# First stage of the transforms in the quarters of TensorE's array, two groups of four matmuls in one visit

## The chip, the cores and the metric

The kernel runs on one core of one Trainium2 chip. The metric is the device time of one execution in microseconds (us), as the median of several runs. TensorE multiplies matrices, ScalarE (ACT) and VectorE (DVE) work on elements, GpSimd (POOL) and SyncE (SP) here mostly issue transfers.

## The reference

For each of 8 batches, x (3008 x 256) is transformed along the sequence, multiplied by a filter and transformed back; then a layer with a leaky activation follows.

```python
X = np.fft.rfft(x, axis=1)
Y = X * (filt_r + 1j * filt_i)[None]
y = np.fft.irfft(Y, n=3008, axis=1)       # 8 x 3008 x 256
h = y.reshape(24064, 256) @ w_in          # 24064 x 2048
g = np.maximum(h, 0) + alpha * np.minimum(h, 0)
out = g @ w_out                           # 24064 x 256
```

## The kernel before, in words

**The transforms.** The length 3008 is split into 47 x 64. A transform (class `Fft`, one for each batch after the first, which `First` does in its own way) has four stages. *Stage a* multiplies by a DFT matrix of length 47 (cosines and sines of 24 frequencies: 48 columns). An x tile `xs` holds a chunk: 8 of the 32 positions of one half of the 64, for both halves h, in 2 x 47 = 94 rows. `piece_a` (L237) is one matmul of 94 rows by 96 columns (a block-diagonal matrix `wf1_s`, one block for each h) over 512 columns of x, into a bank of the pool psF (L245). ScalarE evicts it (`on_act`, L324) into the tile `asb`. Four pieces make a chunk, four chunks a transform, so 7 x 16 = 112 pieces; `save_a` (L249) stores a chunk to `a_dram` from SP, and `turn_a` loads it back turned. *Stage b* (`piece_b`, L265) and the filter (`scale`, L278, with two accumulating transfers on POOL, L281), *stage c* (`piece_c`, L292) and *stage d* (`piece_d`, four matmuls at L317, evicted into `yT`) follow, each in psF banks, two of which alternate (`bank`, L218).

**The layer.** It runs in 47 blocks of 512 rows. `up(j)` (L613), 16 times a block, makes two matmuls of 512 columns (L618; four shorter ones where a block wraps in `yT`) into one half of a tile of the pool `psH` (name hps, two buffers of two banks); after the second of a pair ScalarE evicts both halves at once (L634, 1024 columns), VectorE makes the bent part (`m_s`, L640; ScalarE L638 for one j), and adds it (L821). The second product, `items()`, has two forms. A block whose digit in `KINDS` is a dot takes `eight()`: 64 matmuls of 256 columns (L669). A block with a digit takes `seven()`: seven half-size products in place of eight, 112 matmuls of 128 columns (L691), with sums on VectorE (L650, L652, L658, L594) and some on POOL (L656), and five evictions of 256 columns (L703 to L718). `SUMS` says, for each digit, at which step which sum is made. 38 of the 47 blocks have a digit.

**The order.** It is written out by hand. A step is one `up`. At each step the program emits what is late, the sums, then what `plan` holds for this step (pieces of transforms, stores, loads), then `up(j)`, then as many products of an earlier block as keep the products `LAG` (17) steps behind. `PLACES` holds for each transform the steps of the pieces of a, b, c and d relative to its start (94 steps a batch); `LOADS` those of the loads of x (POOL); `STEPS_*` those of the first transform and of the setup. Each engine works in order, so a piece that waits holds up all that comes after it on its engine.

Of the kernel before, what the change touches and what calls it, by code (L numbers as in the profile page):

```python
# [10 lines left out]
FP16 = mybir.dt.float16  # L11
# [3 lines left out]
N1 = 47  # L15
# [35 lines left out]
)  # L51
STEPS_T = (0, 0, 1, 2, 5, 8, 11, 26, 28, 30, 32, 33)
STEPS_E = (4, 7, 10, 12, 27, 29, 31, 31, 40, 45, 49, 51)
STEPS_N = (34, 37, 38, 23)
STEPS_F = (29, 14, 15, 4, 15)
STEPS_K = (37, 40, 47, 58, 40)
LOADS = (
# [6 lines left out]
)  # L64
KINDS = "...1201.3310001.100000100000001001.00.0000000.."
SUMS = (
# [46 lines left out]
def kernel(  # L113
# [12 lines left out]
    wf1_d = nc.inline_tensor(wf1_np.astype(np.float16), name="c_wf1")  # L126
# [35 lines left out]
    wf1_s = konst.tile([2 * N1, 96], FP16, name="wf1_s")  # L162
# [34 lines left out]
    def load_x(b, c, halves=(0, 1)):  # L197
        if 0 in halves:
            xc[(b, c)] = p_x.tile([2 * N1, 8 * D], FP16, name="xs")
        for h in halves:  # L200
            nc.gpsimd.dma_start(out=xc[(b, c)][h * N1 : h * N1 + N1], in_=xrow(b, h, c))  # L201
# [29 lines left out]
    class Fft:  # L231
# [5 lines left out]
        def piece_a(self, i, evict, wide=False):  # L237
            if i == 0:
                self.at = p_fft.tile([128, NK1, D], FP16, name="at")
            if i % 4 == 0:  # L240
                self.asb[i // 4] = p_as.tile([96, 8, D], FP16, name="asb")
            xs = xc[(self.b, i // 4)]
            ps = bank(wide)
            o = (i % 4) * 512
            nc.tensor.matmul(ps[0:96], wf1_s, xs[:, o : o + 512], start=True, stop=True)  # L245
            u = 2 * (i % 4)
            evict(self.asb[i // 4][:, u : u + 2].rearrange("p a d -> p (a d)"), ps[0:96])

        def save_a(self, c):  # L249
            nc.sync.dma_start(out=a_dram[self.b, :, 8 * c : 8 * c + 8], in_=self.asb[c])  # L250
# [516 lines left out]
    for b in range(1, NB):  # L767
# [3 lines left out]
        for i in range(16):  # L771
            put(p + steps_a[i], f.piece_a, i, on_act)
            if i % 4 == 3:
                put(p + steps_a[i] + (b > 2), f.save_a, i // 4)
# [110 lines left out]
```

## Time and profile before

| | |
|---|---|
| median of 3 runs | 761.08 us (760.99 to 761.57) |
| the profiled execution | 761.13 us, of which 759.3 us span |
| granted TensorE clock | 1.00 |
| matmuls | 7812 |
| stage a: matmuls L245; evictions L324 into asb | 112, 381 ns each; 112, 593 ns each (median) |
| L618 and its evictions L634 | 1600 matmuls; 376 of 1028 ns |
| L691 (seven products), L669 (eight) | 4256 and 512 matmuls |
| VectorE, ScalarE, POOL busy | 694.4, 673.5, 162.9 us |

A row of a group of instructions gives line, engine, operation, output and inputs, shape and count, then busy time, mean duration of one, and the idle time of the engine just before. A matmul's duration holds the latency of the pipeline: from start to start a 512-column matmul takes 0.22 us, though its row says 0.38. The first 34 us are the first transform and the loading of weights; from there the blocks run.

### The profile page before, as it was taken

The page shows a single profiled execution, that of the slowest core. Times are in us where ns is not written, and L with a number is a line of the kernel's source. Part 1 is how long each engine was busy: PE and PEld are TensorE (multiplying, and loading weights), DVE is VectorE, ACT ScalarE, POOL GpSimd, SP SyncE. Part 2 cuts the span into 40 slices and gives each one's busy share as a digit, 9 for nine tenths or more (in the row PEclk, how much of TensorE's full clock was granted, in tenths as well). Part 3 has the DMA queues.
Part 4 walks back from the last instruction along what each step waited for, and adds up shares of the span by engine and source line. Part 5 has one row for each costly group of instructions (what it writes and reads, how often), then busy time and mean ns, then how long its engine had stood idle before and what let it go on. Part 6 is the DMA issues. An engine that isn't in the chain of part 4 may idle for free.

```text
span 759.3 us, 19855 instructions
## 1 busy us (share of the span) xinstructions
PE 743.7 (98%) x7812; PEld 539.3 (71%) x7812; DVE 694.4 (91%) x1298; ACT 673.5 (89%) x1083; POOL 162.9 (21%) x236
## 2 busy tenths in 40 slices
PE   7989999999999999999999999999999999999998
PEld 5746666776787777776778777777777777777766
DVE  5787887998999998899999999999998998999994
ACT  6888999999999998999899998999989898888873
POOL 8631421232022221232022211221100221010100
PEclk9999999999999999999999999999999999999999
DMA  8995888778975596766876659865586355522122
GB/s 158 196 236 157 148 179 217 173 147 167 206 156 118 117 186 172 153 119 142 186 161 144 138 117 204 186 134 115 106 181 137 78 104 113 139 64 65 44 64 62
DMA packets 100790, 107.97 MB, mean 142 GB/s; under 512 B 10568, under 2 KB 81496, under 8 KB 100696
## 3 DMA queue, kind: packets, MB, share of 16 engines
q1 hardware_dynamic: 80136, 70.05, 36.1%
q0 software_dynamic: 20416, 36.58, 29.7%
q8 instruction: 61, 1.00, 0.6%
q14 instruction: 33, 0.27, 0.1%
q10 hardware_dynamic: 144, 0.07, 0.0%
HBM read 55.41 MB, written 46.66 MB: 134 GB/s over the span
## 4 chain that ended last, share of the span: by engine, by line
PE 91%; ACT 1%; DVE 1%; issue 0%; DVEq 0%; ACTq 0%
PE hps L618 42%; PE op L691 31%; PE op L669 7%; PE psF L245 3%; PE psF L317 3%; PE psF L265 2%; PE psF L292 2%; PE op L723 1%; ACT gtb L634 1%; ACT v L324 0%; PE hps L723 0%; DVE m_s L640 0%; ACT asb L324 0%; ACT yT L324 0%; PE psF L426 0%
## 5 line engine op out<-in xcount | busy, mean ns | idle before, releaser
L618 PE MATMUL hps<-yT,win_s 128*128 128x512 f16 (+3 forms) x1600 | 447.6, 366 | 0.4 <-ACT yT L324 0.4
L634 ACT ACTIVATE gtb<-hps 128x1024 f16<-128x1024 f32 x376 | 386.1, 1028 | 50.6 <-PE hps L618 47.8
L691 PEld LDWEIGHTS <-gtb 128*128 128x128 f16 x3040 | 206.0, 98 | 100.0 <-issue 1.0
L640 DVE TENSOR_SCALAR m_s<-gtb,alm_s 128x512 f16<-128x512 f16 x705 | 215.0, 351 | 37.4 <-ACT gtb L634 34.0
L821 DVE TENSOR_TENSOR gtb<-gtb,m_s 128x2048 f16<-128x2048 f16 x188 | 229.8, 1223 | 5.3 <-ACT m_s L638 3.2
L691 PE MATMUL op<-wout_s,gtb 128*128 128x128 f16 x1824 | 153.2, 219 | 0.0
L618 PEld LDWEIGHTS <-win_s 128*128 128x128 f16 x1600 | 135.2, 98 | 24.7 <-issue 3.3
L281 POOL DMA_DIRECT2D uw_s<-uw_s x84 | 72.4, 1002 | 330.4 <-DVE uw_s L278 206.3
L691 PEld LDWEIGHTS <-ss 128*128 128x128 f16 x1216 | 83.1, 98 | 37.4
L691 PE MATMUL op<-tw_s,gtb 128*128 128x128 f16 x1216 | 105.0, 219 | 0.0
L691 PE MATMUL op<-tw_s,ss 128*128 128x128 f16 x1216 | 103.4, 219 | 0.0
L669 PE MATMUL op<-wout_s,gtb 128*128 128x256 f16 x512 | 76.9, 272 | 0.3 <-DVE osb L594 0.3
L656 POOL DMA_DIRECT2D gtb<-gtb x28 | 27.7, 990 | 207.9 <-ACT gtb L634 139.6
L669 PEld LDWEIGHTS <-gtb 128*128 128x128 f16 x512 | 50.0, 98 | 31.3
L324 ACT ACTIVATE asb<-psF 96x512 f16<-96x512 f32 x112 | 65.7, 601 | 1.8 <-PE psF L245 0.9
L324 ACT ACTIVATE yT<-psF 128x376 f16<-128x376 f32 x118 | 56.8, 494 | 5.5 <-PE psF L317 4.6
L324 ACT ACTIVATE v<-psF 128x512 f16<-128x512 f32 x88 | 52.0, 603 | 3.8 <-PE psF L292 2.7
L278 DVE TENSOR_TENSOR uw_s<-uw_s,filt 128x2048 f16<-128x2048 f16 x42 | 51.3, 1221 | 2.9 <-DMA uw_s<-uw_s 2.4
L201 POOL DMA_DIRECT2D xs<-in_x_dram x64 | 51.8, 974 | 5.0 <-issue 2.4
L269 ACT ACTIVATE uw_s<-psF 128x512 f16<-128x512 f32 x84 | 50.0, 605 | 2.9 <-PE psF L265 2.0
L652 DVE TENSOR_TENSOR ss<-ss,gtb 128x1024 f16<-128x1024 f16 x76 | 52.1, 686 | 0.1
L650 DVE TENSOR_TENSOR ss<-gtb 128x1024 f16<-128x1024 f16 (+1 forms) x75 | 52.0, 693 | 0.0
(125 smaller groups left out, 643.7 us busy)
## 6 DMA issues: line engine op xcount, KB each, us to landing
out_dram<-osb SPq DMA_DIRECT2D x127, 128.0 KB
xs<-in_x_dram POOLq DMA_DIRECT2D x64, 188.0 KB, 5.4
a_dram<-asb SPq DMA_DIRECT2D x28, 384.0 KB
uw_s<-uw_s POOLq DMA_DIRECT2D x84, 128.0 KB, 3.6
v_dram<-v SPq DMA_DIRECT2D x112, 96.0 KB
zt<-v_dram SPq DMA_DIRECT2D x28, 384.0 KB
at<-a_dram SPq DMA_DIRECT2D x20, 384.0 KB
gtb<-gtb POOLq DMA_DIRECT2D x28, 256.0 KB, 3.8
```

The costliest lines, as they stand in the source:

```text
L201: nc.gpsimd.dma_start(out=xc[(b, c)][h * N1 : h * N1 + N1], in_=xrow(b, h, c))
L278: nc.vector.tensor_mul(w.rearrange("p (i d) -> p i d", d=1024)[:, 0 : iu // 2 + 1 : iu // 2], uu.unsqueeze(1).to_broadcast([128, 2, 1024]), f)
L281: nc.gpsimd.dma_start(out=uu[o : o + 64], in_=ww[64 - o : 128 - o], accum_op=OP.add)
L324: nc.scalar.activation(o, i, AF.Copy)
L618: nc.tensor.matmul(self.hps[:, j % 2, ca:cb], win_s[:, kt, j * 128 : (j + 1) * 128], yT[:, kt, at : at + cb - ca], start=(kt == 0), stop=( ...
L634: nc.scalar.activation(g, hs, AF.Copy)
L640: nc.vector.tensor_scalar(ms[:, i], g[:, i], 0.0, a, OP.min, OP.mult)
L650: nc.vector.tensor_add(z1, a21, a22)
L652: nc.vector.tensor_add(z2, z1, a11)
L669: nc.tensor.matmul(op[:, si % 2], self.pair(k // 2)[:, k % 2, 128 * si : 128 * si + 128], wout_s[:, k], start=(k == 0), stop=(k == 15))
L691: nc.tensor.matmul(acc[:, 128 * i : 128 * i + 128], x[:, k, 128 * i : 128 * i + 128], b[:, k], start=first and k + i == 0, stop=k == 7, sk ...
L821: nc.vector.tensor_add(g, g, ms)
```

## The change

Stage a is done chunk by chunk. `xs` and the matrix lie in rows 0 to 46 and 64 to 110, one half h in each, and the matrix has 64 columns (48 and 16 of zeros). `piece_a(c)` now makes eight matmuls of 47 rows by 64 columns over 512 columns of x: two groups (j) of four, where each of the four has its own half of the rows (h) and of the columns (u), so that a group covers the four quarters of the array. The first group writes both banks of a tile of psH, the second both banks of psF. ScalarE evicts the first at once (1024 columns), the second in two. All of it is emitted in one visit at the step where the chunk's last piece stood. `asb` has 128 rows; `save_a` stores it with two transfers in place of one. There are 28 visits.

```diff
-    wf1_d = nc.inline_tensor(wf1_np.astype(np.float16), name="c_wf1")
+    wfq_np = np.zeros((2, 64, 64))
+    wfq_np[:, 0:N1, 0:48] = wf1_np[0:N1, 0:48]
+    wf1_d = nc.inline_tensor(wfq_np.reshape(128, 64).astype(np.float16), name="c_wf1")
...
-            nc.gpsimd.dma_start(out=xc[(b, c)][h * N1 : h * N1 + N1], in_=xrow(b, h, c))
+            o = h * (64 if b else N1)
+            nc.gpsimd.dma_start(out=xc[(b, c)][o : o + N1], in_=xrow(b, h, c))
...
-        def piece_a(self, i, evict, wide=False):
-            if i == 0:
+        def piece_a(self, c):
+            if c == 0:
                 self.at = p_fft.tile([128, NK1, D], FP16, name="at")
-            if i % 4 == 0:
-                self.asb[i // 4] = p_as.tile([96, 8, D], FP16, name="asb")
-            xs = xc[(self.b, i // 4)]
-            ps = bank(wide)
-            o = (i % 4) * 512
-            nc.tensor.matmul(ps[0:96], wf1_s, xs[:, o : o + 512], start=True, stop=True)
-            u = 2 * (i % 4)
-            evict(self.asb[i // 4][:, u : u + 2].rearrange("p a d -> p (a d)"), ps[0:96])
+            self.asb[c] = p_as.tile([128, 2, 4, D], FP16, name="asb")
+            hp = psH.tile([128, 2, 512], FP32, name="hps")
+            for j, ps in enumerate(((hp[:, 0], hp[:, 1]), (bank(), bank()))):
+                for u in range(2):
+                    for h in range(2):
+                        r = slice(64 * h, 64 * h + N1)
+                        o = 1024 * u + 512 * j
+                        nc.tensor.matmul(ps[h][64 * u : 64 * u + 64], wf1_s[r], xc[(self.b, c)][r, o : o + 512],
+                                         start=True, stop=True)
+                a = self.asb[c][:, :, 2 * j : 2 * j + 2].rearrange("p h a d -> p h (a d)")
+                if j == 0:
+                    nc.scalar.activation(a, hp, AF.Copy)
+                else:
+                    for h in range(2):
+                        nc.scalar.activation(a[:, h], ps[h], AF.Copy)
 
         def save_a(self, c):
-            nc.sync.dma_start(out=a_dram[self.b, :, 8 * c : 8 * c + 8], in_=self.asb[c])
+            for u in range(2):
+                s = 8 * c + 4 * u
+                nc.sync.dma_start(out=a_dram[self.b, :, s : s + 4].rearrange("(h m) s d -> m h s d", h=2),
+                                  in_=self.asb[c][64 * u : 64 * u + 48])
...
-        for i in range(16):
-            put(p + steps_a[i], f.piece_a, i, on_act)
-            if i % 4 == 3:
-                put(p + steps_a[i] + (b > 2), f.save_a, i // 4)
+        for c in range(4):
+            put(p + steps_a[4 * c + 3], f.piece_a, c)
+            put(p + steps_a[4 * c + 3] + (b > 2), f.save_a, c)
...
-KINDS = "...1201.3310001.100000100000001001.00.0000000.."
+KINDS = "...1....2.10001.100000100000001001.00.0000000.."
```

The order is written anew with it: all of `PLACES`, `STEPS_*`, `LOADS` and `SUMS` have other numbers. The steps of the visits of a transform are the 4th, 8th, 12th and 16th number of its first row; for transforms 1 and 2 (the second starts at step 94) before and after:

```diff
-    ((3, 4, 4, 6, 14, 15, 17, 17, 19, 19, 22, 22, 24, 24, 25, 25),
+    ((0, 0, 0, 0, 1, 3, 3, 4, 5, 9, 10, 12, 16, 17, 17, 20),
...
-    ((-34, -32, -31, -29, -27, -21, -21, -20, -18, -18, -17, -16, -12, -11, -10, -10),
+    ((-73, -63, -54, -52, -49, -39, -32, -28, -21, -21, -20, -20, -20, -17, -17, -15),
...
-     (76, 78, 78, 81, 82, 83, 87, 96, 111, 114, 119, 123, 130, 131, 140, 146)),
+     (77, 77, 79, 80, 84, 101, 102, 104, 106, 110, 112, 125, 127, 142, 144, 146)),
```

The pieces d of transform 1 stand at 80, 80, 80, 80, 82 before and at 80 five times after. Four positions of `KINDS` (4, 5, 6 and 9, counted from 0) turn from digits to dots, so 34 blocks have a digit. Line numbers after: the matmuls of stage a are L249, their evictions L253 and L256, `up` L630 with eviction L646, the products L681 (eight) and L703 (seven), stage d L329.

More of the change, by code (lines that the diff above doesn't have):

```diff
@@ L22 @@
 PLACES = (
[28 rows of a table removed]
-)
[L52 to L56, printed above, removed]
-LOADS = (
[6 rows of a table removed]
[28 rows of a table added]
+)
+STEPS_T = (0, 1, 3, 3, 7, 15, 16, 22, 25, 31, 34, 35)
+STEPS_E = (7, 8, 10, 11, 23, 26, 27, 29, 45, 49, 53, 60)
+STEPS_N = (29, 30, 48, 54)
+STEPS_F = (17, 21, 1, 44, 38)
+STEPS_K = (31, 47, 54, 58, 23)
+LOADS = (
[6 rows of a table added]
 )
-KINDS = "...1201.3310001.100000100000001001.00.0000000.."
+KINDS = "...1....2.10001.100000100000001001.00.0000000.."
 SUMS = (
[4 rows of a table removed]
[3 rows of a table added]
 )
@@ L159 @@
     ctx.enter_context(tc.manual_schedule())
-    wf1_s = konst.tile([2 * N1, 96], FP16, name="wf1_s")
+    wf1_s = konst.tile([128, 64], FP16, name="wf1_s")
     wi3_s = konst.tile([96, 2 * N1], FP16, name="wi3_s")
@@ L198, in load_x @@
         if 0 in halves:
-            xc[(b, c)] = p_x.tile([2 * N1, 8 * D], FP16, name="xs")
+            xc[(b, c)] = p_x.tile([128, 8 * D], FP16, name="xs")
         for h in halves:
-            nc.gpsimd.dma_start(out=xc[(b, c)][h * N1 : h * N1 + N1], in_=xrow(b, h, c))
+            o = h * (64 if b else N1)
+            nc.gpsimd.dma_start(out=xc[(b, c)][o : o + N1], in_=xrow(b, h, c))
     def load_filt(dst, pbase, src, ka, kb):
@@ L344, in piece_a @@
                 o = (4 * sh + u) * D + 128 * f
-                nc.tensor.matmul(ps[:, 96 * u : 96 * u + 96], xc[(0, c)][:, o : o + 128], wfx_s,
+                nc.tensor.matmul(ps[:, 96 * u : 96 * u + 96], xc[(0, c)][0 : 2 * N1, o : o + 128], wfx_s,
                                  start=True, stop=True)
@@ L784 @@
         for q in range(quarters):
-            put(p + steps_a[15] + {3: 3, 4: 7}.get(b, later), f.turn_a, nc.sync, w * q, w * q + w)
+            put(p + steps_a[15] + (7 if b == 4 else later), f.turn_a, nc.sync, w * q, w * q + w)
         for kp in range(12):
```

69 rows, old and new, of tables (LOADS, PLACES, SUMS) are left out of this document.

## The prediction

> **What bounds the kernel now.** First the page's head: the busy line of the engines and the chain that ended last.
>
> ```profile
> span 759.3 us, 19855 instructions
> PE 743.7 (98%) x7812; PEld 539.3 (71%) x7812; DVE 694.4 (91%) x1298; ACT 673.5 (89%) x1083; POOL 162.9 (21%) x236
> ...
> PE 91%; ACT 1%; DVE 1%; issue 0%; DVEq 0%; ACTq 0%
> PE hps L618 42%; PE op L691 31%; PE op L669 7%; PE psF L245 3%; PE psF L317 3%; PE psF L265 2%; PE psF L292 2%; PE op L723 1%; ACT gtb L634 1%; ACT v L324 0%; PE hps L723 0%; DVE m_s L640 0%; ACT asb L324 0%; ACT yT L324 0%; PE psF L426 0%
> ```
>
> TensorE is busy for 98% of the span and is 91% of the chain; the first stage of the transforms (L245) is 3% of it. Because busy time is an average, I then read busy time by stretches (span of the stretch, then PE, PEld, DVE, ACT, POOL).
>
> ```profile
> core 0: us, PE busy (x) PEld busy (x) DVE busy (x) ACT busy (x) POOL busy (x), PEclk, DMA share, GB/s
> 34.00:60.00 26.00, 22.32 (x146) 12.39 (x144) 19.82 (x39) 23.36 (x36) 8.88 (x14) 1.00 0.98 213
> 60.00:90.00 30.00, 30.00 (x247) 21.64 (x244) 26.13 (x49) 25.49 (x38) 9.13 (x12) 1.00 0.72 157
> 90.00:125.00 35.00, 32.39 (x287) 21.89 (x285) 28.16 (x50) 32.95 (x56) 8.27 (x11) 1.00 0.86 198
> 125.00:200.00 75.00, 74.97 (x754) 53.20 (x751) 67.75 (x125) 71.39 (x119) 17.10 (x23) 1.00 0.84 173
> 200.00:300.00 100.00, 100.00 (x1096) 73.40 (x1094) 97.01 (x183) 93.00 (x152) 19.15 (x25) 1.00 0.72 158
> ```
>
> From 125 us on TensorE has no idle time at all and the granted clock is 1.00. There, time is what TensorE streams, plus any wait that the change creates. Only 34 to 60 us (3.7 us idle) and 90 to 125 us (2.6 us idle) have something to give back, and there ScalarE is busy for 90% and 94%. Who was waited for in these stretches:
>
> ```profile
> PE psF L317 <- DVE zt L327: 1.7, 1, 1.7
> PE psF L245 <- ACT asb L324: 0.8, 2, 0.6
> PE psF L317 <- ACT yT L324: 0.8, 2, 0.5
> PE hps L618 <- ACT yT L324: 0.4, 1, 0.4
> PE psF L245 <- ACT yT L324: 0.4, 1, 0.4
> PE psF L245 <- DVE yT L327: 0.2, 1, 0.2
> ```
>
> **The change, part by part.** The chain in order of time gives the cost of a matmul as start to start, without the pipeline's latency (start, duration, what):
>
> ```profile
> 76.26 0.44 PE op L669 x4
> ...
> 130.00 0.22 PE psF L245
> ...
> 134.72 0.43 PE hps L618 x2
> ...
> 135.15 0.45 PE op L691 x8
> ```
>
> (1) *What goes.* 112 matmuls of 512 columns (L245) at 0.22: 24.6 us.
>
> (2) *What comes: streaming.* 28 visits of eight matmuls. The nearest rows are matmuls into the two column halves of the array at the start (L489, 64 columns of weights each); the last two rows give the time of one matmul.
>
> ```profile
> 11.02 0.33 PE L345 MATMUL op<-idx_s,xs 94*128 94x96 f16 x4 [0.32 <-DVE gtb L327]
> 11.28 0.64 PE L489 MATMUL hps<-idx_s,ss 128*64 128x128 f16 x16
> 11.85 0.34 PE L345 MATMUL psF<-idx_s,xs 94*128 94x96 f16 x4
> ...
> L345 PE MATMUL op<-idx_s,xs 94*128 94x96 f16 x32 | 2.7, 206 | 0.3 <-DVE gtb L327 0.3
> L489 PE MATMUL hps<-idx_s,ss 128*64 128x128 f16 x32 | 1.3, 222 | 0.0
> ```
>
> The last of the sixteen starts at 11.28 + 0.64 - 0.22 = 11.70, so eight pairs start within 0.42 us, a pair every 0.06: the cost of one full matmul of 128 columns (0.45 / 8). Two halves do run side by side. Going in: the last L345 before starts at 11.02 + 0.33 - 0.21 = 11.14, the first half-array matmul 0.14 later where 0.04 is usual: 0.10 lost. Going out: 11.85 - 11.70 = 0.15 where 0.05 is usual: 0.10 lost. So I estimate an undisturbed visit at 2 x 0.22 + 0.10 + 0.10 + 0.01 = 0.65 us against 0.88: 28 x 0.23 = 6.4 us less. Quarters by rows don't occur in this trace; the bounds are all four side by side (0.65) and all eight in a row (8 x 0.22 + 0.20 = 1.96).
>
> The Trainium skill (TensorEngine Tiling (Array Packing), Key Properties) says that a change of the tiling mode drains TensorE, and gives no duration. The two 0.10 us above agree with it; without the drain an undisturbed visit would be 0.45 us, and the result below would be the same.
>
> (3) *What comes: a wait.* The first group of a visit takes a tile of the pool hps, which has two buffers and otherwise serves only the pairs of L618. The visit stands between the pair Z and the next pair A. Before, A took the buffer of the pair before Z; now the visit has taken that one, and A takes Z's own, so A's first matmul waits until ScalarE has evicted Z (L634). Two places of the trace show how long that is:
>
> ```profile
> 548.56 0.59 PE L618 MATMUL hps<-yT,win_s 128*128 128x512 f16 x2
> 549.00 0.44 PE L691 MATMUL op<-wout_s,gtb 128*128 128x128 f16 x5
> 549.27 0.28 PE L691 MATMUL op<-tw_s,gtb 128*128 128x128 f16 x2
> 549.38 0.59 PE L618 MATMUL hps<-yT,win_s 128*128 128x512 f16 x2
> ...
> 549.25 1.01 ACT L634 ACTIVATE gtb<-hps 128x1024 f16<-128x1024 f32 x1
> ```
>
> ```profile
> 227.93 0.60 PE L618 MATMUL hps<-yT,win_s 128*128 128x384 f16 x4
> ...
> 228.76 0.33 PE L317 MATMUL psF<-wi_s,zt 96*128 96x94 f16 x4
> 228.93 0.60 PE L618 MATMUL hps<-yT,win_s 128*128 128x384 f16 x4
> ...
> 228.57 1.02 ACT L634 ACTIVATE gtb<-hps 128x1024 f16<-128x1024 f32 x1 [0.25 <-PE hps L618]
> ```
>
> In the first, the eviction ends at 550.26, 0.88 after the next pair began. In the second, ScalarE waited for TensorE (228.53 to 228.57, a hand-over of 0.04); its eviction ends at 229.59, 0.66 after the next pair began, and 0.17 of other matmuls stood between. With 0.04 to hand back, TensorE can fill 0.92 and 0.87 us between the products of L691 and A. An undisturbed visit fills 0.65 of that. **So each visit costs about 0.89 us, whatever the array does, and 0.24 of it is a wait**: 28 x 0.89 = 24.9, against 24.6 before: +0.3 us. Behind the waiting matmul stands everything else on TensorE, as it works in order; ScalarE's next eviction and VectorE behind it wait for that.
>
> The first three visits come before step 17, where no products (0.39 a step by the rows above) stand between Z and the visit: 3 x 0.39 = +1.2. The waits that L245 had (0.8 + 0.4 + 0.2) go: -1.4. Together -0.2.
>
> (4) *Four blocks lose the product of seven.* In KINDS the positions 4, 5, 6 and 9 turn from digits to dots; a block has then 64 matmuls of L669's kind for 112 of L691's: 64 x 0.44 / 4 = 7.04 against 112 x 0.45 / 8 = 6.30. 4 x 0.74 = **+3.0 us**, all on TensorE. Other engines gain:
>
> ```profile
> L652 DVE TENSOR_TENSOR ss<-ss,gtb 128x1024 f16<-128x1024 f16 x76 | 52.1, 686 | 0.1
> L658 DVE TENSOR_TENSOR gtb<-gtb,ss 128x2048 f16<-128x2048 f16 (+1 forms) x38 | 45.8, 1206 | 0.0
> L708 ACT ACTIVATE osb<-op 128x256 f32<-128x256 f32 x38 | 15.1, 397 | 0.0
> L674 ACT ACTIVATE osb<-op 128x512 f32<-128x512 f32 x16 | 9.5, 594 | 0.2 <-PE op L669 0.2
> ```
>
> VectorE loses some 5 us of sums a block, ScalarE 5 x 0.40 - 2 x 0.59 = 0.8. Positions 4 to 6 lie in and behind the stretch of 90 to 125 us. I let that return 1.6 of its 2.6 us idle: **-1.6** (bounds 0 and -2.6).
>
> (5) *ScalarE's evictions.* They come as 1024 + 512 + 512 columns, where four of 512 stood:
>
> ```profile
> L634 ACT ACTIVATE gtb<-hps 128x1024 f16<-128x1024 f32 x376 | 386.1, 1028 | 50.6 <-PE hps L618 47.8
> L324 ACT ACTIVATE asb<-psF 96x512 f16<-96x512 f32 x112 | 65.7, 601 | 1.8 <-PE psF L245 0.9
> ```
>
> 1.03 + 2 x 0.60 = 2.23 against 2.40, but in one lump. Steady pairs follow each other by 2 x (0.43 + 0.39) = 1.64, so in the first place above the evicted buffer was wanted again at 549.38 + 1.64 = 551.02, 0.8 after its eviction; the lump uses that up and no more. I take 0; if some ten visits spill by 0.3, it is +3. One visit is worse: the last of transform 2 stands at the odd step 79, between the halves of a pair, with five pieces of L317 at step 80. These need banks that come free behind the lump, the pair's eviction and their own (0.5 each). By the sums above TensorE would be there after 2.3 us and ScalarE after 5.3; four such pieces cost 0.8 + 0.4 before. I take **+1.0** (0 to 1.8).
>
> (6) *Transfers.* The store of a chunk becomes two halves on SP (28 more issues) with rows of half the length; loads of x are moved. From 125 us on the DMA share is 0.84 and 0.72, and no row of the waits names a store or a load of x; cost 0. Where this cover is missing, at 34 to 60 us with 0.98, it may be +1.
>
> Sum: 0.3 - 0.2 + 3.0 - 1.6 + 1.0 = +2.5. The profiled execution took 761.13 (759.3 of span and 1.8 around it), as good as the median 761.08. Forecast: **763.6 us**.
>
> **Rivals.** *A, no wait on the buffer.* If A finds its buffer free, a visit is 0.65 and the time 763.6 - 28 x 0.24 = **756.9**, faster. For it: TensorE streams that much less. Against: the two places above, in both of which ScalarE followed the pair closely. It breaks even with before when a visit takes 0.80 us instead of 0.89. The Trainium skill (TensorE: Matmul & The Clock Gate, Part 3, Measured speedup vs the span model) has a group of side-by-side matmuls take one matmul and 4 ns per further tile; the pairs of L489 agree. That is this rival's time for a visit, once nothing holds A.
>
> *B, the early stretches give more.* ScalarE bounds them and loses work. If 3.2 us of the 6.3 come back, and step 79 costs nothing: **761.0**, no difference.
>
> *C, the quarters run two by two.* A visit is 4 x 0.22 + 0.20 = 1.08, over the 0.89, so 28 x 0.19 = 5.3 more: **768.9**. *D, they don't overlap at all:* 1.96 a visit, **793.6**: the change then doesn't do what it says. Against both: halves overlap fully at L489; row quarters are untried in this trace.
>
> **How the numbers follow.** Forecast 0.48 (761 to 766), A 0.17, B 0.17, C 0.13, D 0.05. A measurement of this kernel tells about 0.2% (1.5 us) from no change. Faster: A and a third of B, 0.23. Same: the rest of B and the lower end of the forecast, 0.20. Slower: 0.57. The range 757.0 to 769.0 reaches to A and C, and leaves out half of A, D and little else.
>
> **What will show it.** In the profile after: L630 waiting for L646 some 28 times, about 0.24 each (A: not at all); matmuls of L249 in fours starting within some 20 ns, fours 0.22 apart (C, D: twos, ones); 34 x 112 = 3808 matmuls of L703; the idle time of TensorE in 90 to 125 us near 1 us, with a wait of 2 us or more behind step 79. I am wrong if A's wait is absent, or if ScalarE falls behind after most visits.

## The result and the profile after

| | before | after |
|---|---|---|
| median | 761.33 us (760.99 to 762.45) | 772.66 us (769.2 to 774.31) |
| ratio, 95% interval | | 1.014 (1.0104 to 1.0177) |
| profiled execution, its span | 761.13, 759.3 | 772.72, 771.0 |

The change makes the kernel slower by 1.4%: 11.6 us between the profiled executions, where 2.5 were forecast. The time lies outside the range. That it is slower, as forecast, is luck: the terms that made the forecast +2.5 (the dots and step 79) are not what the runs show the loss to be. First the head of the page of after.

```profile
span 771.0 us, 19623 instructions
PE 744.9 (97%) x7732; PEld 534.7 (69%) x7732; DVE 673.5 (87%) x1265; ACT 672.5 (87%) x1043; POOL 159.2 (21%) x233
...
PEclk9999998999999999999999999999999999999999
```

TensorE is busy for 744.9 us where it was 743.7, while the span is 11.7 us longer: what was lost is time in which TensorE waits, and time in which it works at a lower clock (that counts as busy). The one 8 in the clock's row says where to look. Busy time by stretches, after, then before:

```profile
88.00:96.00 8.00, 5.76 (x33) 3.40 (x31) 7.81 (x15) 4.03 (x7) 4.07 (x7) 0.79 0.78 145
96.00:135.00 39.00, 34.10 (x306) 22.96 (x305) 25.15 (x48) 32.77 (x53) 7.42 (x11) 0.91 0.80 183
```

```profile
88.00:96.00 8.00, 7.53 (x56) 5.28 (x55) 5.61 (x10) 7.44 (x13) 2.78 (x4) 1.00 0.96 167
96.00:135.00 39.00, 36.86 (x354) 24.92 (x353) 31.49 (x57) 36.70 (x63) 7.56 (x10) 1.00 0.85 201
```

From 88 to 135 us TensorE is idle for 7.1 us of 47 (2.6 before) and its clock is 0.79 and 0.91. Since both kernels make the same 752 steps of `up`, the start of each step in the two traces tells where the time went (after minus before):

| step | 0 | 48 | 56 | 72 | 80 | 88 | 136 | 272 | 744 |
|---|---|---|---|---|---|---|---|---|---|
| us | +0.8 | +0.4 | +3.7 | +2.3 | +6.7 | +8.5 | +9.4 | +12.9 | +11.3 |

Two spots make most of it: steps 48 to 56 (about 83 to 95 us) and 72 to 88 (112 to 137 us), both before the second transform's stage d. From step 272 to the end, with 11 of the visits, after is the faster one, by 1.6 us; why was not traced. The waits of TensorE, longest first:

```profile
PE hps L630 <- ACT gtb L646: 3.0, 16, 0.5
PE psF L329 <- DMA zt<-v_dram: 2.8, 2, 1.8
...
PE op L681 <- DVE gtb L832: 2.2, 1, 2.2
PE psF L304 <- ACT v L336: 1.8, 1, 1.8
PE psF L304 <- DMA uw_s<-uw_s: 1.0, 1, 1.0
```

The forecast's wait is there (the first row), but small. The chain in order of time (start, duration, what) shows both spots. Spot 1:

```profile
81.32 5.95 DMA filt<-filt
...
87.72 0.69 DVE tw_s L813
88.40 0.66 DVE m_s L652 x2
...
89.68 1.24 DVE gtb L832
...
90.96 0.73 PE op L681 x4
91.69 0.85 PE psF L304 x4
92.55 0.85 PE hps L630 x2
```

This view follows the copy of some filter rows (`swapped`, planned for step 44), which lands at 87.3. But what VectorE stood still for is another transfer of the same queue (rows of VectorE, POOL and SP):

```profile
86.58 1.23 DVE L290 TENSOR_TENSOR uw_s<-uw_s,filt 128x2048 f16<-128x2048 f16 x1 [3.30 <-DMA uw_s<-uw_s]
...
79.70 1.79 POOL L293 DMA_DIRECT2D uw_s<-uw_s  x2 [2.85 <-ACT asb L256]
80.78 1.81 POOL L773 DMA_DIRECT2D filt<-filt  x2
...
79.88 0.80 SPq L261 DMA_DIRECT2D a_dram<-asb  x2
```

The scaling L290 waits 3.30 us for the accumulating transfer of the scaling before it, which is issued at 80.24 and lands at 86.45; the copy is issued right behind it, and the store of the visit at step 42 (L261) beside it. Behind the scaling stands the addition L832, and TensorE's products L681 wait for that. Nothing on VectorE waited for the copy itself: the instruction that needs it (L769) starts at 89.09. Then a pair of L630 takes 0.85 where it takes 0.43: TensorE runs at half clock. Spot 2:

```profile
106.35 1.23 DVE uw_s L290
...
108.42 5.84 DMA uw_s<-uw_s
...
114.31 0.41 PE psF L304 x2
...
121.08 5.97 DMA zt<-v_dram
...
127.10 0.49 PE psF L329 x4
127.59 0.85 PE hps L630 x2
128.45 0.75 PE op L703 x7
```

This is the tail of transform 1: the last scaling, its accumulating transfer, stage c, the store of v, the load zt, stage d at the fixed step 80. TensorE is there early and waits; again half clock follows. In the kernel before the last scaling begins at 103.20 and stage d at 120.12, 16.9 us; here it is 106.35 to 127.10, 20.7 us. So stage d is 7.0 us later: 3.2 because the chain starts later, and 3.8 because it is longer. Of these 3.8, 1.6 lie between the issue of the last accumulating transfer and its landing (4.2 before, 5.8 here), the rest behind it.

### The profile page after: what moved, and what is told of

It reads as the page before. It is cut to its first block, busy times and chain, and to the rows that moved or that the text cites. A ratio compares the mean times of both kernels' runs of the same rounds, so it can differ in the third digit from the quotient of the medians.

```text
span 771.0 us, 19623 instructions
## 1 busy us (share of the span) xinstructions
PE 744.9 (97%) x7732; PEld 534.7 (69%) x7732; DVE 673.5 (87%) x1265; ACT 672.5 (87%) x1043; POOL 159.2 (21%) x233
## 4 chain that ended last, share of the span: by engine, by line
PE 83%; ACT 7%; DMA 5%; DVE 2%; issue 2%; POOL 1%; SPq 0%; ACTq 0%; DVEq 0%
PE hps L630 39%; PE op L703 26%; PE op L681 9%; ACT gtb L646 4%; PE psF L329 2%; PE psF L304 2%; PE psF L277 2%; DMA uw_s<-uw_s 2%; DMA win_s<-in_moe_w_in_dram 1%; DMA zt<-v_dram 1%; DMA filt<-filt 1%; DVE gtb L832 1%; PE op L735 1%; PE hps L376 1%; DMA uw_s<-c_twp 0%
## 5 line engine op out<-in xcount | busy, mean ns | idle before, releaser
L630 PE MATMUL hps<-yT,win_s 128*128 128x512 f16 (+3 forms) x1600 | 448.6, 368 | 4.8 <-ACT gtb L646 3.0
L646 ACT ACTIVATE gtb<-hps 128x1024 f16<-128x1024 f32 x376 | 388.1, 1033 | 55.5 <-PE hps L630 52.0
L703 PEld LDWEIGHTS <-gtb 128*128 128x128 f16 x2720 | 185.2, 98 | 89.6 <-issue 1.4
L832 DVE TENSOR_TENSOR gtb<-gtb,m_s 128x2048 f16<-128x2048 f16 x188 | 228.7, 1217 | 6.2 <-ACT m_s L650 3.2
L630 PEld LDWEIGHTS <-win_s 128*128 128x128 f16 x1600 | 134.5, 98 | 26.0 <-issue 11.6
L703 PE MATMUL op<-wout_s,gtb 128*128 128x128 f16 x1632 | 136.6, 219 | 0.5 <-DVE gtb L832 0.5
L681 PE MATMUL op<-wout_s,gtb 128*128 128x256 f16 x768 | 116.0, 274 | 2.2 <-DVE gtb L832 2.2
L681 PEld LDWEIGHTS <-gtb 128*128 128x128 f16 x768 | 75.3, 98 | 50.9 <-DVE gtb L832 2.7
L703 PEld LDWEIGHTS <-ss 128*128 128x128 f16 x1088 | 74.5, 98 | 33.6
L703 PE MATMUL op<-tw_s,gtb 128*128 128x128 f16 x1088 | 94.8, 220 | 0.0
L703 PE MATMUL op<-tw_s,ss 128*128 128x128 f16 x1088 | 93.0, 219 | 0.0
L290 DVE TENSOR_TENSOR uw_s<-uw_s,filt 128x2048 f16<-128x2048 f16 x42 | 51.1, 1217 | 16.5 <-DMA uw_s<-uw_s 11.3
L668 POOL DMA_DIRECT2D gtb<-gtb x26 | 26.6, 1024 | 174.9 <-ACT gtb L646 110.7
L664 DVE TENSOR_TENSOR ss<-ss,gtb 128x1024 f16<-128x1024 f16 x68 | 46.3, 682 | 0.0
L662 DVE TENSOR_TENSOR ss<-gtb 128x1024 f16<-128x1024 f16 (+1 forms) x67 | 46.1, 689 | 0.0
L329 PE MATMUL psF<-wi_s,zt 96*128 96x94 f16 x496 | 40.7, 206 | 3.4 <-DMA zt<-v_dram 2.8
```

What stands on the lines that cost most here:

```text
L290: nc.vector.tensor_mul(w.rearrange("p (i d) -> p i d", d=1024)[:, 0 : iu // 2 + 1 : iu // 2], uu.unsqueeze(1).to_broadcast([128, 2, 1024]), f)
L329: nc.tensor.matmul(ps[:, m], self.zt[g][:, 4 * mh + m, dh * 128 : dh * 128 + 128], wi3_s, start=True, stop=True)
L630: nc.tensor.matmul(self.hps[:, j % 2, ca:cb], win_s[:, kt, j * 128 : (j + 1) * 128], yT[:, kt, at : at + cb - ca], start=(kt == 0), stop=( ...
L646: nc.scalar.activation(g, hs, AF.Copy)
L681: nc.tensor.matmul(op[:, si % 2], self.pair(k // 2)[:, k % 2, 128 * si : 128 * si + 128], wout_s[:, k], start=(k == 0), stop=(k == 15))
L703: nc.tensor.matmul(acc[:, 128 * i : 128 * i + 128], x[:, k, 128 * i : 128 * i + 128], b[:, k], start=first and k + i == 0, stop=k == 7, sk ...
```

## The experiments

The theory after the first look: the visits cost what was forecast, and the loss lies in the order that was written with them, at the two spots. The rival: the visits themselves, by their wait and by ScalarE's lump of evictions. (Beside after, before's own median was 761.3; beside the other runs it was 762.0 to 763.3, so the ratios compare better than the times.)

**The visit.** The first run puts the products of the step between a visit and the next pair.

```diff
-            blk.up(j)
+            if not visit:
+                blk.up(j)
             while todo and done < (step - LAG) / 16:
...
+            if visit:
+                blk.up(j)
```

> The changed kernel, but at a step with a visit the products (L703 or L681) are emitted between the visit and the next pair, so that the wait for the eviction of the pair before is filled. If that wait is 0.24 us at some 24 visits, as the prediction has it: 5 to 6 us less than the changed kernel, 766 to 768 where that one gives 772. If something else sets a visit's 0.88 us (the drain of the array, the weights): no difference.

Measured: 770.19 (767.5 to 771.0), ratio 1.0096 (1.0072 to 1.012). TensorE's instructions around one visit, in after and then in this run:

```profile
256.61 0.33 PE L703 MATMUL op<-tw_s,gtb 128*128 128x128 f16 x3
256.87 0.41 PE L249 MATMUL hps<-xs,wf_s 47*64 47x512 f16 x4
257.11 0.39 PE L249 MATMUL psF<-xs,wf_s 47*64 47x512 f16 x4
257.67 0.59 PE L630 MATMUL hps<-yT,win_s 128*128 128x512 f16 x2 [0.17 <-ACT gtb L646]
```

```profile
255.91 0.41 PE L249 MATMUL hps<-xs,wf_s 47*64 47x512 f16 x4
256.15 0.39 PE L249 MATMUL psF<-xs,wf_s 47*64 47x512 f16 x4
256.47 0.56 PE L703 MATMUL op<-tw_s,gtb 128*128 128x128 f16 x7
256.87 1.03 PE L630 MATMUL hps<-yT,win_s 128*128 128x512 f16 x4
```

The four quarters start within 10 ns of each other (four matmuls in 0.41, one takes 0.40), the second four 0.24 later. In after the next pair begins 0.80 after the visit's first matmul; with 0.09 that are lost going in, a visit costs 0.89. With the products between it is 0.56 + 0.09 = 0.65, and the wait is gone. So both of the forecast's figures for a visit are right. Of the 20 late visits' 20 x 0.23 = 4.6 us some 2.5 were kept by the medians, whose intervals overlap, and 2.0 in the traces from step 96 on. A new wait of products for VectorE's sums (L703 for osb L606, 1.1 us in three) took back some; the rest was not traced.

Next, the same visits at the same steps with the old matmuls, four of 94 rows and 96 columns, two in hps and two in psF.

```diff
-                        nc.tensor.matmul(ps[h][64 * u : 64 * u + 64], wf1_s[r], xc[(self.b, c)][r, o : o + 512],
+                nc.tensor.matmul(ps[u][0:96], wf1_s, xc[(self.b, c)][0 : 2 * N1, o : o + 512], start=True, stop=True)
```

> The changed kernel with the same visits and the same places of the evictions, but four matmuls of 94 rows by 96 columns over the whole array instead of two groups of four in the quarters (two into the tile of hps, two into psF), and one store for a chunk. A visit is 4 x 0.22 = 0.88 us on TensorE, then the eviction of the pair before is over: within 1 us of the changed kernel. If the quarters save what they stream (0.23 us a visit): 6 us slower; if their stores of half length do harm: faster.

Measured: 768.05 (763.97 to 771.35), ratio 1.0069 (1.0046 to 1.0091). One of its visits:

```profile
253.42 0.60 PE L245 MATMUL hps<-xs,wf_s 94*96 94x512 f16 x2
253.85 0.59 PE L245 MATMUL psF<-xs,wf_s 94*96 94x512 f16 x2
254.30 0.59 PE L622 MATMUL hps<-yT,win_s 128*128 128x512 f16 x2
```

0.88 from the visit's first matmul to the next pair: without quarters a visit costs the same. From step 160 to the end, with 16 visits, the distance to after stays between 3.2 and 3.5 us, so there visits by quarters cost what visits of the whole array cost. But the run is 4.6 us faster than after, where I expected 1 us at most; "faster" was named as the sign that the stores of half length do harm. Its gain lies at spot 1: steps 48 to 56 lose nothing (3.2 in after), though the copy of the filter rows stands where it stood. There the accumulating transfer takes 4.5 us from issue to landing, not 6.2. Whether the stores' form does it, or that they fall a little earlier, no run tells apart.

**Order and form.** One run takes the new order with the old first stage, one the new first stage with the old order (each visit at the even step at or before its old one), one this with the products between.

> The new tables (PLACES, STEPS, LOADS, KINDS, SUMS) with the old first stage: 112 matmuls of 94 rows by 96 columns, each at its own step of the new first row. Theory O (the loss lies in the new order, at two places near steps 56 and 80, and in the half clock behind them): 768 to 774. Theory V (the lump of a visit, its evictions and its two stores make stages c and d late): only the four blocks without seven products remain, 763 to 765.

Measured: 800.23, ratio 1.0494 (1.0464 to 1.0523). The largest part is four waits of stage a for x, 13.0 us in all: the new tables' loads of x are made for visits, and the single pieces, which use numbers of the row that after never reads, come before them. The run doesn't answer the question.

> The old tables with the new visits, each at the even step at or before that of the chunk's last piece. Theory O: a visit costs 0.89 us as four pieces did, so 760 to 764. Theory V: the late stages come back with the visits, 767 to 772.

Measured: 777.49, ratio 1.0186 (1.0158 to 1.0214). Here the loss grows with the visits, to +17 in the profiled run: stages b, c and d stand beside many visits and wait for banks behind the lump of evictions (waits of L250, L278, L305 and L330 for ScalarE, 0.4 to 0.8 us at a time). So in the old order the visits do cost, and there the rival is right.

> The old tables with the new visits and the products between the visit and the next pair. Theory O with the filled wait: 0.65 us a visit for 0.88, 28 x 0.23 = 6 us less than before: 754 to 757, faster than both kernels. Theory V: 762 to 768.

Measured: 779.71, ratio 1.0222 (1.02 to 1.0245): nothing is won. The wait for the tile of hps (4.2 us in e2) is gone from the longest waits, but stages still wait for banks of psF (L305 for the lump 2.6, L250 for stage b 2.5), and products for VectorE's sums (L704, 1.5).

**Spot 1.** The last copies of filter rows at steps 22 and 23.

```diff
-STEPS_F = (17, 21, 1, 44, 38)
+STEPS_F = (17, 21, 1, 22, 23)
```

> The changed kernel, but two of the four copies of filter rows (the third and the fourth number behind STEPS_F's first two) are issued at steps 22 and 23 instead of 44 and 38. If the stall of TensorE at 88 to 92 us comes from the copy of step 44, on which VectorE's scaling waits and behind it the sums that the products need, that stall (2.4 us) and the half clock after it (3.4 us at half speed, 1.7 us) go: 768 to 770 where the changed kernel gives 772.5. If the lump of the visits makes it: no change.

Measured: 768.37 (767.8 to 769.5), ratio 1.0078 (1.0063 to 1.0093), 4.3 us less than after, as expected. Step 56 starts 2.7 us earlier than in after, step 80 only 1.0: from step 72 to 88 the run loses 7.1 us, after 6.2.

That looks like the price of the copy, but the other traces say that the copy alone doesn't make it. I took the time from issue to landing of the accumulating transfer of spot 1 in all twenty, and counted the packets of the visit's store that ran beside it. It is 3.5 to 5.1 us where at most 41 ran beside it, and 5.9 to 7.4 where 112 or more did: in after, e3, e7, e16 and e18 with the copy behind it on the queue, in e9 and e10 with a load of x there instead. In e11 below, with the copy at the same step and no store, it is 4.5, and steps 48 to 56 lose nothing. In e5 the store falls earlier against the transfer (41 packets beside it, 125 in after), so e5 doesn't separate the two. No run moves this store alone.

**The four blocks without the product of seven.**

```diff
-KINDS = "...1....2.10001.100000100000001001.00.0000000.."
+KINDS = "...1534.2610001.100000100000001001.00.0000000.."
```

> The changed kernel with the digits of before at positions 4, 5, 6 and 9 of KINDS, each with its own row of sums. By step (4) of the prediction 3.0 us less of products on TensorE; if the relief of VectorE and ScalarE was worth 1.6 as forecast, 771; if it was worth nothing, because the chain of transform 1 bounds that stretch: 769.5 or less.

Measured: 774.6 (773.1 to 777.4), ratio 1.0162. With the four products of seven back it is no faster; the waits show why:

```profile
PE op L707 <- DVE osb L610: 3.3, 5, 1.1
```

VectorE's sums come too late for five of the products. So in this order, with the sums at the places tried here, the digits win nothing; whether other places would give the 3.0 us back was not tried.

**Spot 2, by the tables.** Four runs move single things ahead of step 80: stages b and c of transform 1 earlier at their end (e6), the loads of x at the steps of before (e9; with the products between, e10), transform 2's visits at 42, 48, 52 and 56 in place of 42, 66, 74 and 79 (e12). All stand on e5.

> e5, and in addition the last two pieces of stage b and the last five of stage c of transform 1 three steps earlier (63, 64 to 60, 61; 68 to 73 to 65 to 70). If the wait at step 80 (4 us, and 6.8 us at half clock behind it) is the latency of the chain b, scaling, accumulating transfer, c, store, load, d, against the fixed step 80: most of it goes, 762 to 765. If the burst of a visit's stores makes the load of zt late: 768 to 770, as e5.

> e5, and the loads of x for transforms 2 and 3 that stood at steps 62, 50, 32 and 55, 77 go to steps 47, 37, 43 and 80, 88, so that none is issued between the accumulating transfers of transform 1's stage b from step 53 on. If these loads (376 KB a chunk, on the same queue) make the last accumulating transfers land after 5 to 6.6 us instead of 3, and with them stages c, the store and the load of zt late for step 80: 762 to 765 where e5 gives 768. If the length of the chain itself or the visits' stores make it late: 767 to 769.

> e9 with the products between the visit and the next pair, as in e3, which took 2.5 us off the changed kernel (4.6 us of waits for the eviction went, and about half came back as waits for VectorE): 2 to 3 us less than e9. Under the theory of the loads 760 to 762, at before's time; otherwise 765.

> e5, with the visits of transform 2 at steps 42, 48, 52, 56 instead of 42, 66, 74, 79 (their loads of x earlier to match, the turned load of stage a where it was), so that no visit stands between the last scaling of transform 1 (step 64) and step 80. If the lumps and stores of these visits make stage c, the store of v and the load of zt late: the wait of 3 to 4 us at step 80 goes and with it the half clock, 762 to 765 where e5 gives 768. If the chain is late by itself, or the visits only do their harm earlier: 767 to 770.

Measured: 771.82 (ratio 1.0116), 771.88 (1.0128), 769.27 (1.0086) and 770.3 (1.0101), none better than e5's 768.37, except that the products between again save 2.6 beside e9. Step 80 stays 126 to 129 us into the span in all of them. The wait only moves along the chain of transfers, here in e6 and e12:

```profile
PE psF L304 <- DMA uw_s<-uw_s: 3.2, 2, 1.8
```

```profile
PE psF L329 <- DMA zt<-v_dram: 3.2, 1, 3.2
```

My theory about the loads of x was hardly put to the test: POOL runs ahead of the steps, so the steps of its loads order its queue and little else. In e9 the load planned for step 80 is issued at step 68, again right behind the last accumulating transfer of transform 1, and another (at 81.1 us) stands behind the transfer of spot 1, where steps 48 to 56 now lose 4.5 us.

Three runs mix the kernels: before, with the new setup tables (`STEPS_N`, `STEPS_F`, two rows of `LOADS`); after, with transforms 1 and 2 in the old form, places and digits (e14), and this with the products between (e15).

> The kernel before, old first stage and old places, with only the new order of the filter copies (STEPS_N, STEPS_F) and of the first eight loads of x (the first two rows of LOADS). No visit is in it. Theory of the order: its early stretch loses what the changed kernel loses there, 4 to 9 us over before, 766 to 771. If the visits are needed to make the stretch late: within 1.5 us of before.

> A mixture: transforms 1 and 2 with the first stage, the places, steps and digits of the kernel before, transforms 3 to 7 with the visits and the places of the changed kernel. If all of the loss but some 2.5 us lies in the stretch of transforms 1 and 2, as the step-by-step difference of the traces says: 763 to 765. If visits cost anywhere: 767 or more.

> e14 with the products between the visit and the next pair. The 20 late visits lose their 0.23 us of waiting, half of which came back as waits for VectorE in e3: 2 us less than e14, 760.5 to 763, level with before.

Measured: 767.21 (1.0064, interval 1.0028 to 1.0101), 771.44 (1.0116) and 771.66 (1.0117). The first has no visit in it and loses 4.4 us by step 88, with waits for transform 1's transfers (L317 for zt 2.0, L292 for uw_s 1.8) and 3.4 us of half clock. The setup alone can thus cost 4 us, most of it at spot 2 and none at spot 1. The second is equal to before up to step 88 (+0.14), at a clock of 1.00, then loses 4.4 by step 136 and 8.8 by step 272, where old and new places stand side by side; with the products between (e15) nothing is won. I had expected 763 to 765, and 767 or more "if visits cost anywhere", which is what came. The waits of that stretch are for ScalarE (L270 for yT 1.5, L325 for v 1.5) and for transfers (L325 for uw_s 1.4); whether the visits or the mixture make them is not shown. So e14 shows that the loss at step 80 is not a matter of the later visits, and the rival is not excluded.

**Spot 2, by its parts.** Is it the wait, or the half clock behind it? Matmuls that nobody reads fill TensorE's idle time.

```diff
+    def busy(n):
+        hp = psH.tile([128, 2, 512], FP32, name="hps")
+        for _ in range(n):
+            nc.tensor.matmul(hp[:, 0, 0:128], id16, id16, start=True, stop=True)
+
+    put(73, busy, 24)
+    put(80, busy, 64)
```

> The changed kernel with 24 matmuls of 128 columns that nobody reads at step 73 (ahead of the third stage) and 64 at step 80 (ahead of the fourth), about 0.056 us each by like rows, 1.3 + 3.6 us: they stand where TensorE otherwise waits for the late transfers of transform 1. Theory that the drop to half clock (6.8 us at 0.5 from 125.4 us, 3.4 us of work) follows TensorE's own idling: the idle time is filled, the granted clock stays near 1.00 from 96 to 135 us, step 88 starts some 3 us earlier than in the changed kernel, and the time is 769 to 770, though work was added. Rival, that the clock drops for another reason, or that the wait for the transfers alone sets the time: the slices stay at 0.5 for as long, or the time is 772 to 774.

Measured: 770.25 (768.61 to 770.92), ratio 1.0104 (1.0083 to 1.0125), 2.4 less than after by the medians, with overlapping intervals and 88 matmuls more. The stretches:

```profile
88.00:96.00 8.00, 5.79 (x44) 4.24 (x45) 7.70 (x16) 5.66 (x10) 4.17 (x8) 1.00 0.78 139
96.00:135.00 39.00, 35.86 (x391) 25.96 (x389) 26.05 (x48) 31.67 (x52) 6.70 (x10) 1.00 0.82 189
```

The clock is 1.00 throughout (in the profiled execution; the other three have means of 0.997 and 0.998): where the idle time is filled, at spot 2, no half clock follows. But from step 72 to 88 the run loses 6.7 us, after 6.2. What the full clock gives there, the 64 matmuls take, which hold back the first three pieces of stage d though their rows had come; the last packet of zt lands at 126.05, 1.5 us earlier than in after, while TensorE is 2.3 us earlier at step 72. The trace's 3.0 us against after are 1.6 at spot 1, where the same wait (L681, 2.3) is this time not followed by half clock, 0.8 that are there before it, and 1.4 between steps 136 and 272, less 0.6 at spot 2.

> The changed kernel with the copies of the filter rows at steps 22 and 23 (768.4 alone), the products between a visit and the next pair (770.2 alone), and the same idle matmuls at steps 73 and 80. If the three parts are separate losses, their savings add: 4.3 + 2.5 + 3 off 772.7, 763 to 765. If they share one loss, the wait for transform 1's transfers, which takes back what is won ahead of it, the time stays at 766 to 769. In neither case is it under the kernel before (761.3).

Measured: 767.27 (766.01 to 767.89), ratio 1.0071 (1.005 to 1.0092). The savings don't add to 763 to 765: they share the wait.

What makes the transfers late? The packets in the trace show the last scaling's accumulating transfer (two halves, 128 packets) taking 2.75 us from the first to the last packet in before, and 4.55 in after. SP's queue of after around it:

```profile
106.94 2.94 SPq L598 DMA_DIRECT2D out_dram<-osb  x3
109.99 0.88 SPq L261 DMA_DIRECT2D a_dram<-asb  x2
111.01 6.63 SPq L313 DMA_DIRECT2D v_dram<-v  x8
120.66 1.60 SPq L322 DMA_DIRECT2D zt<-v_dram  x3
```

The transfer runs from 109.3 to 113.8, and the store of the visit at step 66 (L261, behind three stores of results) runs beside it. Over the runs so far, it took 2.0 to 3.5 us where no such store lay beside it, or five packets of one (before, e1, e2, e4, e11, e12, e14, e15), and 3.7 to 5.5 where one did (after, e3, e5 to e10, e16, e17). So one run moves that visit to step 64, and one takes all parts together, with the idle matmuls divided among the pieces of stage d (8, 24, 24).

```diff
-    ((-73, -63, -54, -52, -49, -39, -32, -28, -21, -21, -20, -20, -20, -17, -17, -15),
+    ((-73, -63, -54, -52, -49, -39, -32, -30, -21, -21, -20, -20, -20, -17, -17, -15),
```

> The changed kernel with one visit moved: the second of transform 2 from step 66 to step 64, so that its store stands on SP's queue ahead of the three stores of results. Theory that this store, lying beside the last accumulating transfer of transform 1, slows it: that transfer's packets took 2.75 us from the first to the last in the kernel before, 2.7 to 3.1 where no such store lay beside it, 3.8 to 5.5 (4.55 in the changed kernel) where one did; it should fall to 2.7 to 3.5, step 80 should start 1 to 2 us earlier, and the time be 770.5 to 772. Rival, that the transfer is slow for another reason: it stays at 4 to 5.5 us and the time at 772 to 774.

> The copies of the filter rows at steps 22 and 23, the products between a visit and its pair, the visit at step 64, and the idle matmuls divided: 24 at step 73, and at step 80 8, 24 and 24 ahead of the first three pieces of the fourth stage instead of 64 ahead of all, which held the first pieces back though their rows had come. Without the store beside the last transfer 1 to 2 us, and by the divided matmuls some 1.5 us less than 767.3: 764 to 765.5, if the wait at step 80 is what remains; 766 to 768 if it is not.

Measured: 770.2 (769.69 to 771.2), ratio 1.0108 (1.0093 to 1.0123), and 765.49 (765.06 to 765.53), ratio 1.0043 (1.0026 to 1.006). In e18 step 80 starts 1.5 us earlier, but the accumulating transfer still takes 4.5: the store, though two steps earlier, was issued at 106.0 and still ran beside it, so this run says nothing on the store. In e19 the store comes early enough, and the transfer takes 2.94:

```profile
103.45 0.78 SPq L261 DMA_DIRECT2D a_dram<-asb  x2
104.97 2.21 SPq L598 DMA_DIRECT2D out_dram<-osb  x3
107.43 8.14 SPq L313 DMA_DIRECT2D v_dram<-v  x8
117.35 1.26 SPq L322 DMA_DIRECT2D zt<-v_dram  x3
```

It runs from 107.4 to 110.3. e19 differs from e17 in more than the store, so that the store is the cause is likely and not proved. Nor is it the whole of spot 2: in e12 and e19, where the transfer is fast, steps 72 to 88 still lose 4.6 us each, against 6.2 in after. e19 is 0.43% slower than before and the best of the new kernels; no version beat the one before. Its 4.1 us at the end (profiled runs) arise at step 80: TensorE is 0.75 us early at step 72 and 4.5 late at step 80, and the last packet of zt lands at 123.96, against 120.91 in before.

## Why the prediction was wrong, by its steps

By the table of steps the 11.3 us are 2.3 up to step 72 (spot 1 alone 3.2), 6.2 at spot 2, 0.9 up to step 136, 3.5 up to step 272, and -1.6 from there on. The forecast had a gain of 1.6 where spot 2 lies, and nothing for transfers. My list of who was waited for in before lacks the longest wait between 90 and 125 us, for an accumulating transfer of transform 1:

```profile
PE psF L292 <- DMA uw_s<-uw_s: 0.8, 1, 0.8
```

- *Steps (1) to (3), the visit:* right. 0.65 undisturbed and 0.89 with the wait were forecast; both were measured (e3, after). The whole-array visits of e8 cost 0.88 as well, as "whatever the array does" says. The wait's row shows 16 waits and 3.0 us where 28 of 0.24 were expected: 15 of 0.17 behind products of seven and one of 0.49. (The row counts from the end of the matmul before, which holds the latency; from start to start the 0.17 are 0.24, as e3 shows.) Seven visits behind products of eight wait 0.12 each, too short for the row, and five hardly or not at all.
- *Step (4), the dots, +3.0:* not confirmed. Putting the digits back gains nothing (e7), but their sums then come too late; what the dots cost in this order stays open.
- *Step (4), the relief, -1.6, and step (6), transfers 0:* **the steps that failed, in the same place.** "I let that return 1.6 of its 2.6 us idle", with bounds 0 and -2.6: idle time was taken for something that less work gives back. Of before's 2.6 us from 90 to 125 us, 1.6 are waits for ScalarE and 0.8 the wait above. In after TensorE is idle there for 4.6 us, where I expected 1; its waits are 2.2 at spot 1, 2.8 for zt and uw_s, and only 0.5 for ScalarE (some reach over the ends of the stretch). And what is won ahead of step 72 waits at step 80: e17 and e19 are 1.2 and 0.75 us early at the one and 5.5 and 4.5 late at the other. The chain of transfers got 3.8 us longer in place of staying the same, a loss of 6.2 us from step 72 to 88, where the forecast had a gain. The bound of 0 excluded a loss without a reason. And "no row of the waits names a store" was read from before, where no store of a visit ran beside the accumulating transfers of transform 1. In after one does at each spot, and there they take 6.2 and 5.8 us from issue to landing where they took 4.3 and 4.2. That the stores do it is likely and not proved; that TensorE waits for these transfers, at spot 1 behind VectorE and at spot 2 behind the rest of the chain, with 3.2 and 6.2 us lost there, the half clock counted in, the traces show.
- *What the sum had no term for:* the copies of filter rows moved to step 44. The diff shows `STEPS_F` and `STEPS_N` rewritten, and my step (6) looked at the stores and the loads of x alone. Moving them gave 4.3 us (e5); without a visit's store beside it the same copy costs nothing there (e11). And the half clock behind each wait: 3.4 us long at spot 1, 6.8 at spot 2, which costs up to half of that.
- *Step (5), +1.0 for the odd step 79:* a wait of 2 us or more behind it was named as the sign, and it came (L329, 2.8 in two), but for zt and not for banks behind the lump of evictions. The visit itself took 0.65 there.
- *The rivals:* A's condition, a free buffer, didn't come about; when e3 makes it so, 2.5 us return, not 6.7. B was the opposite of what happened: the early stretches lost. C and D are out: the quarters overlap fully.
- *Later on:* +3.5 from step 136 to 272, of which 1.8 is one wait of stage c for ScalarE (L304 for v) and 0.74 the dot at position 9; the rest is small and I didn't trace it.

Open is why the first of the five accumulating transfers of that tail starts 1.7 us later than before in after and e19 (81.6 against 79.9), and why zt's packets take 5.9 and 5.7 us there where they took 4.8. e11 shows that the setup tables alone make some of the loss at spot 2; which of their rows was not tried.

## What to carry to other kernels

A stage whose results return through memory at a fixed step is timed by its transfers, so a relief of the engines ahead of it was worth nothing here, and a transfer that is moved beside one of them has to be asked for its price; the tables of transfers in a diff are to be costed like instructions. Before costing a faster way through an engine, look for the buffer that the next instruction needs: here it came free some 0.89 us after the products, so a visit of 0.65 and one of 0.88 cost the same. A short idle time of TensorE can cost more than itself: behind the 2.2 us at spot 1 came 3.4 us at half clock.

## What the runs showed of the hardware

*Half clock.* In after the granted clock falls to 0.5 for 3.41 us from 91.33 and for 6.83 us from 125.46, twice the first. Busy time in the 3.41 us ahead of each:

```profile
87.92:91.33 3.41, 1.17 (x12) 0.63 (x11) 3.35 (x7) 1.74 (x3) 2.79 (x4) 1.00 0.67 124
122.05:125.46 3.41, 1.20 (x20) 0.92 (x19) 1.30 (x4) 3.05 (x6) 0.00 (x0) 1.00 0.93 255
```

In e16 the same wait of 2.3 us falls on two such windows:

```profile
85.97:89.38 3.41, 1.96 (x17) 1.15 (x14) 3.35 (x6) 2.90 (x5) 2.03 (x4) 1.00 0.48 107
89.38:92.79 3.41, 2.58 (x20) 1.94 (x21) 3.31 (x7) 1.49 (x3) 0.76 (x2) 1.00 0.93 138
```

and the clock stays full. (Its windows are counted in steps of 3.413 us from its first change of clock, as the clock changes inside every run lie whole such steps apart.) Over the twenty traces, counted in such windows, half clock followed every window in which TensorE was busy for 1.57 us or less and none above 2.0; between, it went both ways (e5 lost the clock after 1.99 us). Whether an idle time of about 2 us costs something thus depends on where it falls: of after's own runs, one with a mean clock of 0.998 took 769.2 us, the profiled one with 0.993 took 772.7. The Trainium skill (TensorE: Matmul & The Clock Gate, Part 1: The HAM clock gate) describes a free-running window of 3413 ns and half rate after an idle one; the lengths and the phase agree, but here the windows ahead of the drops were busy for a third of their time, not idle.

*Quarters.* Four matmuls of 47 rows and 64 columns run side by side in the time of one (0.41 us for the four, 0.40 for one); the change into the quarters costs 0.09 us (the first starts 0.15 after the last product, where 0.06 is usual).

*Queues.* POOL's loads start when its queue lets them, well ahead of their step (step 68 for one planned for step 80, in e9); a visit's store on SP waits behind three stores of results, 2.9 us in after.
